# Attention, slot routing and a gated layer on one core: the first state link and its scaling are issued first in an iteration, the gate weights' scaled words right behind them on ScalarE

## The chip, the core and the metric

The kernel runs on one core of one Trainium2 chip. A core has five engines that run side by side, each through its own list in order: TensorE (PE, with its weight loads as PEld), VectorE (DVE), ScalarE (ACT), GpSimd (POOL) and SyncE (SP), which here issues nearly all loads. Engines wait for each other by semaphores. The metric is device microseconds of one execution; the time of before is the median of three runs.

## The reference, cut to what matters

```python
for t in range(S):                      # B=4, H=8, S=768, D=48
    state = alpha[:, :, t, :, None] * state + einsum('bhd,bhe->bhde', k[:, :, t], v[:, :, t])
    y[:, :, t] = einsum('bhd,bhde->bhe', q[:, :, t], state)
...
x = y laid out as (B * S, H * D)        # 3072 x 384
logits = x @ phi                        # 8 experts of 4 slots each: 32 columns
d = softmax of logits over tokens;  slot_input = d.T @ x
slot_out[e] = relu(slot_input[e] @ w1[e]) @ w2[e]
x = softmax of logits over slots @ slot_out
...
out = (silu(x @ w_gate) * (x @ w_val)) @ w_out      # float64 weights in memory
```

The weights of the last layer arrive as 64-bit floats, so the kernel has to make 32-bit floats of them from their words.

## The kernel before, in words

The work is in three stages. The first is a loop over `g` from 0 to 31 in the function `fast`: 16 pairs of heads (`n`), each in two halves (`h`) of three chunks of 128 tokens. The state of a pair is carried from chunk to chunk by a chain: TensorE adds the old state to a chunk's own product by a product with the identity (the **link**, L402 in `emit_st`), and ScalarE multiplies the sum by the chunk's decay and writes the new state to SBUF (the **scaling**, L404). The next link reads what the scaling wrote. An iteration holds two links that stand near its start (`emit_st(g, 1 - h)` and `emit_st(g, 2 - h)`); between them stand the score products of the next half (`emit_s`, L353, twelve passes). In odd iterations a third is issued later.

Around that chain an iteration does this. VectorE runs two decay scans for the half three further on (L306 to L314 in `scan_w` and `scan_p`) and masks the next half's scores (L360 in `emit_masks`). GpSimd scales keys and queries (L325) and masks the other head's scores (L363). ScalarE copies keys (L374), tokens (L466), scores (L362) and the output of the half (L434 in `emit_ip`). TensorE also adds the past's and the half's own part of the output (L420, L432) and forms logits (L453). The scores lie in two PSUM banks that are used again in each iteration, so the score products of an iteration need the masks and copies of the one before.

Into the same loop the conversion of the 24 gate-weight parts is woven, one part an iteration: `conv_y` (ScalarE, L249, the **scaled words**) writes a scratch of 128x384; VectorE makes the number of it in three steps, `conv(0)` (L253), `conv(1)` (L257, reads the scratch) and `conv(2)` (L261, reads it last). A part is loaded one or two iterations ahead (`pump_gv`, L244). Iterations 0, 1, 11, 12, 19, 20, 27 and 28 have none. A batch is four pairs of heads, so eight iterations; behind its end ScalarE also takes exponentials of the logits and copies them (L488, L490, L494 in `slot_steps`). They are issued at the end of iterations 8, 16 and 24, behind L434, and so stand ahead of the words and the first scaling of iterations 9, 17 and 25.

Everything is issued in the order in which the code is written; there is no scheduler. Each engine keeps that order. Loads go out on SyncE in the order of the calls, and a load into a region waits until its last reader is done. After the loop come the slot routing and experts (L853, L910), fed by weight loads (L236) into memory that the loop frees, and then the last layer (L1006 to L1045).

Of the kernel before, what the change touches and what calls it, by code (L numbers as in the profile page):

```python
# [34 lines left out]
GV0, RATE = 1, 840  # L35
# [57 lines left out]
def attention_slots_mlp(ctx: ExitStack, tc: tile.TileContext, kq, at, vt, phi, w1, w2, wgv, wo, cst, out):  # L93
# [47 lines left out]
    def program(general):  # L141
# [30 lines left out]
        def view(r, rows=128):  # L172
            o = r[0] % FAR
            return (near_t if r[0] < FAR else far_t)[0:rows, o:o + r[1]]

        def drop(r):
            ar.free(*r)
# [27 lines left out]
        def pump_units(limit=100):  # L205
            while uloads and limit:
                limit -= 1
                nm, i = uloads[0]
                z, n = {"a": (z_a, HW), "p": (z_p, HB), "v": (z_v, 288)}[nm]
                if not z:  # L210
                    return
                r = have[uloads.pop(0)] = (z.pop(0), n)
                if nm == "v" or i > 1:
                    load_unit(nm, i, r)

        def load_unit(nm, g, r):
            n, h = sgs[g]
            if nm == "a":
                nc.sync.dma_start(out=view(r), in_=at[units[n]][:, 387 * h:387 * h + HW])
            elif nm == "v":  # L220
                nc.sync.dma_start(out=view(r), in_=vt[units[n]][:, 288 * h:288 * h + 288])
            else:
                nc.sync.dma_start(out=view(r), in_=kq[units[n]][:, HB * h:HB * h + HB])
# [23 lines left out]
        def to_f32_y(raw, i=0):  # L247
            y = view(z_c[i])
            nc.scalar.activation(y, raw[:, 1::2], AF.Copy, scale=2.0 ** -112)  # L249
            return y  # L250
# [24 lines left out]
        def conv_y():  # L275
            i = gvd[0]
            if i < NG and ("wgv", divmod(i, 4)) in have:
                gvy[i] = to_f32_y(view(have["wgv", divmod(i, 4)]))
# [23 lines left out]
        def scan_w(g, between=lambda: None):  # L302
            n, h = sgs[g]
            wreg[g] = ((z_w.pop(0), HW), have.pop(("a", g)))
            w, a = (view(x, 112) for x in wreg[g])
            nc.vector.memset(rst[:, ::129], 1.0)  # L306
            nc.vector.tensor_tensor_scan(w[:, ::-1], a[:, ::-1], rst[:, ::-1], 0.0, ALU.mult, ALU.add)  # L307
            between()
            nc.vector.tensor_tensor(out=tots[:, n, 3 * h:3 * h + 3], in0=w[:, 1:387:129], in1=least, op=ALU.max)  # L309
            nc.vector.reciprocal(rst[:, 0:387:129], tots[:, n, 3 * h:3 * h + 3])  # L310
# [5 lines left out]
        def scale(g, which, eng):  # L316
            o = 2 - which
            if not which:
                pair[g] = have.pop(("p", g))
                kp[g], qp[g] = ((pair[g][0] + x, 384) for x in (0, 384))  # L320
            xv = view((kp, qp)[which][g], 112).rearrange("p (c t) -> p c t", t=CH)
            r = wreg[g][which]
            sv = view(r, 112)[:, o:o + 1]
            sv = bass.AP(sv.tensor, sv.offset, [list(sv.ap[0]), [129, 3], [1, CH]])
            eng.tensor_tensor(out=xv, in0=xv, in1=sv, op=ALU.mult)  # L325
            if g + (2, 4)[which] < NSG:
                (z_w, z_a)[which].append(r[0])
            else:
                drop(r)
# [6 lines left out]
        def nk(g):  # L336
            return 3 if sgs[g][1] == 0 else 2
# [39 lines left out]
        def new_g():  # L377
            ng[0] += 1
            return gsts[:, ng[0] % 7, :]
# [15 lines left out]
        def emit_st(g, c):  # L395
            if c >= nk(g):
                return
            n, h = sgs[g]
            cc = 3 * h + c + 1
            ps = dps[g][0:112, c * 48:c * 48 + 48]  # L400
            for p in (slice(0, 64), slice(64, 112)) if cc > 1 else ():
                nc.tensor.matmul(dps[g][p, c * 48:c * 48 + 48], lhsT=ident[p, p], rhs=gst[n, cc - 1][p, 0:48], start=False, stop=True, skip_group_check=True)  # L402
            gst[n, cc] = new_g()
            nc.scalar.mul(gst[n, cc][:, 0:48], ps, tots[:, n, cc:cc + 1])  # L404
            if c == nk(g) - 1:
                del dps[g]
# [164 lines left out]
        def keep_warm(n, p=None):  # L571
            if p is None:
                p = ps_y.tile([128, 512], F32, tag="y", name="warm")
            for _ in range(n):
                nc.tensor.matmul(p, lhsT=cold[0][:, 0:128], rhs=cold[0], start=True, stop=True)

        def fast():
            pump_units(4)

            def first_loads(h):  # L580
                for nm in "ap":
                    load_unit(nm, h, have[nm, h])

            first_loads(0)
            nc.scalar.dma_start(out=cs, in_=cst[:, 0:289])
            first_loads(1)
            nc.scalar.dma_start(out=phs, in_=phi)
            pump_units()
            calm, cold[0] = cold[0], view((z_g[0], 256)).bitcast(BF16)
            nc.gpsimd.memset(cold[0], 0.0)  # L590

            keep_warm(10)
            cold[0] = calm
            nc.vector.memset(rst, 0.0)
            nc.vector.memset(least, TINY)
            nc.gpsimd.memset(gsts, 0.0)
            scan_w(0)
            scale(0, 0, nc.gpsimd)
            scan_p(0)
            scale(0, 1, nc.vector)  # L600
            for c in range(3):
                emit_s(0, c)
            emit_kt(0)
            del kp[0]
            scan_w(1)
            scale(1, 0, nc.gpsimd)
            scan_p(1)
            keep_warm(4)
            scale(1, 1, nc.vector)
            emit_masks(0)  # L610
            emit_dh(0)
            emit_st(0, 0)
            pump_units()
            scan_w(2)
            scan_p(2)
            scale(2, 0, nc.gpsimd)
            scale(2, 1, nc.vector)
            pump_units()
            keep_warm(6)
            pend = []  # L620
            credit[0] = 0
            for g in range(NSG):
                n, h = sgs[g]
                nxt = g + 1 < NSG
                if g + 3 < NSG:
                    scan_w(g + 3, lambda: conv(0))
                    scan_p(g + 3)
                else:
                    conv(0)
                if g and g + 2 < NSG:  # L630
                    scale(g + 2, 0, nc.gpsimd)
                    scale(g + 2, 1, nc.gpsimd)
                conv(1)

                emit_st(g, 1 - h)
                if nxt:
                    for c in range(3):
                        emit_s(g + 1, c)
                emit_st(g, 2 - h)
                if nxt:  # L640
                    emit_kt(g + 1)
                if g:
                    emit_xt(g - 1)
                if nxt:
                    emit_masks(g + 1)
                    del kp[g + 1]
                    pump_units()
                late = False
                if g:
                    emit_l(g - 1)  # L650
                    release(xt.pop(g - 1), z_x, g + 1)
                    p = sgs[g - 1][0]
                    if sgs[g - 1][1] == 1 and units[p][1] == NU - 1:
                        pend += slot_steps(units[p][0])
                        late = True
                        pend.pop(0)()
                if pend and not late:
                    pend.pop(0)()
                emit_past(g)
                if nxt:  # L660
                    emit_dh(g + 1)
                    if h:
                        emit_st(g + 1, 0)
                conv(2)
                emit_ip(g)
                if late:
                    pend.pop(0)()
                    pend.pop(0)()
                if GV0 <= g and (g < 8 or g % 8 not in (2, 3)):
                    conv_y()  # L670
                if gvd[0] == NG and z_c:
                    done_c()

                pump_gv()
                credit[0] = min(credit[0] + RATE, 2 * BLK)
                reserve[0] = 6 - len(gvb)
                while credit[0] > 0:
                    c = credit[0]
                    pump(1)
                    if credit[0] == c:  # L680
                        break
                pump_units()
            for r in z_t:
                drop(r)
            assert few[1] is not None
            pump()
# [495 lines left out]
```

## Time and profile before

| | |
|---|---|
| median of 3 runs | 394.04 us (393.09 to 395.3) |
| the profiled execution | 395.87 us, its span 394.1 us |
| busy: TensorE, weight loads | 372.6 us (95%), 278.1 us (71%) |
| busy: VectorE, ScalarE, GpSimd | 291.0 us (74%), 201.5 us (51%), 103.9 us (26%) |
| mean granted clock of TensorE | 0.986 |

The profile is one execution. The span goes from the first to the last instruction; the time has 1.8 us more around it. Busy shares are means over the whole span, and the three stages differ, so a stage has to be cut out before a share says anything about it. The loop's 32 iterations take from some 13 to 158 us. In the rows, PEld is TensorE's weight load, which is where a wait of a product shows first; an arrow in brackets names the instruction that ended an engine's idle time.

### The profile page before, as it was taken

How to read it: one execution, taken by the hardware profiler on the slowest of the kernel's cores; microseconds unless marked ns; L12 is line 12 of the kernel's file. 1: busy time of each engine (PE TensorE's matmuls, PEld its weight loads, DVE VectorE, ACT ScalarE, POOL GpSimd, SP SyncE). 2: the span in 40 equal slices, each digit the busy share in tenths (PEclk: the TensorE clock that was granted, in tenths of full speed). 3: DMA queues.
4: the chain of work that ended last, by engine and by line, in shares of the span. 5: the costliest groups of instructions: out<-in, count | busy, mean ns of one | idle time of the engine just before them, and what ended most of it. 6: DMA issues, size and time to landing. Idle time of an engine off the chain costs nothing.

```text
span 394.1 us, 8610 instructions
## 1 busy us (share of the span) xinstructions
PE 372.6 (95%) x3309; PEld 278.1 (71%) x3309; DVE 291.0 (74%) x566; ACT 201.5 (51%) x468; POOL 103.9 (26%) x105
## 2 busy tenths in 40 slices
PE   6999999998998998999799999999999999999992
PEld 3677767776776776434358868888888888888781
DVE  6999997997999773214598995767767877877550
ACT  1456665656466455423267655446445445446431
POOL 3378675788588741020300000000000000000000
PEclk8999999999999999999899999999999999999997
DMA  8899997999799849799900004104114114112002
GB/s 277 316 320 360 351 360 276 312 346 321 258 362 351 289 157 350 288 335 407 400 33 0 1 2 150 39 34 150 35 37 151 37 35 148 39 35 81 2 1 89
DMA packets 28627, 74.25 MB, mean 188 GB/s; under 512 B 3216, under 2 KB 11648, under 8 KB 28576
## 3 DMA queue, kind: packets, MB, share of 16 engines
q1 hardware_dynamic: 28256, 73.27, 52.3%
q8 instruction: 28, 0.46, 0.5%
q10 hardware_dynamic: 272, 0.21, 0.2%
q14 instruction: 23, 0.19, 0.1%
q0 software_dynamic: 48, 0.13, 0.1%
HBM read 68.87 MB, written 4.72 MB: 187 GB/s over the span
## 4 chain that ended last, share of the span: by engine, by line
PE 55%; DVE 6%; DMA 3%; ACT 3%; issue 2%; SPq 0%; DVEq 0%; ACTq 0%
PE m L1045 21%; PE acc L1045 11%; PE s L1006 4%; PE s L1007 4%; DMA near<-w 3%; PE s L853 3%; PE y L432 2%; PE y L420 2%; DVE near L1012 1%; DVE rnd L1020 1%; ACT near L249 1%; PE sw L975 1%; PE l L453 1%; PE m L402 1%; PE m L390 1%
## 5 line engine op out<-in xcount | busy, mean ns | idle before, releaser
L1045 PE MATMUL m<-rnd 128*128 128x512 f32 x432 | 129.2, 389 | 0.0
L1045 PEld LDWEIGHTS m<-rnd 128*128 128x128 f32 x432 | 81.1, 188 | 16.8
L1009 ACT ACTIVATE near<-s 128x512 f32<-128x512 f32 x72 | 43.1, 599 | 79.0 <-PE s L1006 77.3
L1045 PE MATMUL acc<-rnd 128*128 128x512 f32 x216 | 81.1, 392 | 0.8 <-DVE rnd L901 0.8
L325 POOL TENSOR_TENSOR far<-far 112x384 f32<-112x384 f32 x61 | 78.5, 1306 | 6.5 <-DVE tots L309 3.6
L1012 DVE TENSOR_TENSOR near<-near,s 128x512 f32<-128x512 f32 x72 | 49.4, 686 | 36.1 <-ACT near L1009 35.9
L1020 DVE TENSOR_TENSOR rnd<-near,rnd 128x512 fp32r<-128x512 f32 x72 | 49.4, 686 | 3.2 <-ACT rnd L1018 3.1
L1045 PEld LDWEIGHTS acc<-rnd 128*128 128x128 f32 x216 | 40.5, 188 | 10.3 <-DVE rnd L901 1.6
L1018 ACT CAST rnd<-near 128x512 fp32r<-128x512 f32 x72 | 44.3, 615 | 0.2 <-DVE near L1012 0.2
L404 ACT ACTIVATE far<-m,tots 112x48 f32<-112x48 f32 x80 | 24.1, 301 | 29.1 <-PE m L402 17.3
L307 DVE TENSOR_TENSOR_SCAN far<-far,r 112x388 f32<-112x388 f32 x32 | 30.8, 962 | 5.2 <-DMA far<-at 2.5
L353 PE MATMUL s<-far 64*128 64x128 f32 x384 | 30.6, 292 | 2.5 <-DVE r L306 2.1
L1116 DVE TENSOR_REDUCE amm<-near 112x1 f32<-112x768 f32 x32 | 30.3, 947 | 2.5 <-DMA near<-at 2.5
L363 POOL TENSOR_SCALAR_AFFINE_SELECT far<-far 128x384 f32<-128x384 f32 x32 | 19.1, 596 | 48.8 <-ACT far L362 48.8
L314 DVE TENSOR_TENSOR_SCAN far<-far,r 112x387 f32<-112x387 f32 x32 | 30.7, 959 | 1.1
L257 DVE SCALAR_TENSOR_TENSOR near<-near 128x384 uint32<-128x384 uint32 x36 | 24.2, 672 | 7.9 <-ACT near L249 7.0
L434 ACT COPY far<-y 112x384 f32<-112x384 f32 x32 | 15.3, 480 | 28.1 <-PE y L432 28.1
L432 PE MATMUL y<-far 128*48 128x128 f32 (+1 forms) x384 | 28.6, 274 | 0.0
L1006 PE MATMUL s<-rnd 128*128 128x512 f32 x72 | 28.3, 393 | 0.0
L1007 PE MATMUL s<-rnd 128*128 128x512 f32 x72 | 28.1, 391 | 0.0
L353 PEld LDWEIGHTS s<-far 64*128 64x128 f32 x384 | 24.4, 189 | 4.7 <-POOL far L325 2.6
L402 PE MATMUL m<-far,cs 64*64 64x48 f32 (+1 forms) x256 | 19.9, 229 | 6.5 <-ACT far L404 3.8
(163 smaller groups left out, 495.0 us busy)
## 6 DMA issues: line engine op xcount, KB each, us to landing
near<-w SPq DMA_DIRECT2D x18, 768.0 KB, 6.8
far<-kq SPq DMA_DIRECT2D x32, 384.0 KB, 4.8
far<-w SPq DMA_DIRECT2D x14, 768.0 KB, 6.7
near<-wgv SPq DMA_DIRECT2D x24, 384.0 KB, 5.4
far<-at SPq DMA_DIRECT2D x32, 194.0 KB, 4.7
near<-at SPq DMA_DIRECT2D x16, 339.1 KB, 3.3
far<-vt SPq DMA_DIRECT2D x32, 144.0 KB, 4.0
near<-wo SPq DMA_DIRECT2D x12, 384.0 KB, 8.7
```

What stands on the lines that cost most here:

```text
L307: nc.vector.tensor_tensor_scan(w[:, ::-1], a[:, ::-1], rst[:, ::-1], 0.0, ALU.mult, ALU.add)
L314: nc.vector.tensor_tensor_scan(a, a, rst[:, 0:387], 0.0, ALU.mult, ALU.add)
L325: eng.tensor_tensor(out=xv, in0=xv, in1=sv, op=ALU.mult)
L353: nc.tensor.matmul(sps[g][s][:, o:o + CH], lhsT=k[64 * s:64 * s + 64, t0:t0 + CH], rhs=q[64 * s:64 * s + 64, t0:t0 + CH], start=True, stop ...
L432: nc.tensor.matmul(ps[p, o], lhsT=v[:, c, 48 * s:48 * s + p.stop - p.start], rhs=smk[g, s][:, c], start=False, stop=True, skip_group_check ...
L1006: nc.tensor.matmul(pg, lhsT=swk[n][:, 128 * o:128 * o + 128], rhs=ctT[t % 4], start=True, stop=True)
L1007: nc.tensor.matmul(pv, lhsT=swk[n][:, 256 + 128 * o:256 + 128 * o + 128], rhs=ctT[t % 4], start=True, stop=True)
L1009: nc.scalar.activation(sg, pg, AF.Silu)
L1012: nc.vector.tensor_tensor(out=h_, in0=sg, in1=pv, op=ALU.mult)
L1018: nc.scalar.copy(hi, h_)
L1020: nc.vector.tensor_tensor(out=lo, in0=h_, in1=hi, op=ALU.subtract)
L1045: nc.tensor.matmul(p, lhsT=passes[j][0][:, sl], rhs=passes[j][1], start=(f == 0 and j == 0), stop=(f == NF - 1 and j == 2))
```

## The change

In an iteration of the loop, `emit_st(g, 1 - h)` (the first link and its scaling) is called first, ahead of the scans, the scalings of keys and queries and the conversion steps, which are for other engines. `conv_y` is called right behind it instead of at the end of the iteration before; the conditions are shifted by one, so the same iterations have words as before.

```diff
             for g in range(NSG):
                 n, h = sgs[g]
                 nxt = g + 1 < NSG
+
+                emit_st(g, 1 - h)
+                if GV0 < g and (g <= 8 or g % 8 not in (3, 4)):
+                    conv_y()
                 if g + 3 < NSG:
                     scan_w(g + 3, lambda: conv(0))
                     scan_p(g + 3)
...
                     scale(g + 2, 0, nc.gpsimd)
                     scale(g + 2, 1, nc.gpsimd)
                 conv(1)
-
-                emit_st(g, 1 - h)
                 if nxt:
                     for c in range(3):
                         emit_s(g + 1, c)
...
                 if late:
                     pend.pop(0)()
                     pend.pop(0)()
-                if GV0 <= g and (g < 8 or g % 8 not in (2, 3)):
-                    conv_y()
                 if gvd[0] == NG and z_c:
                     done_c()
```

The order of TensorE, VectorE, GpSimd and SyncE is the same in both kernels. Only ScalarE's differs, at 24 places. The first piece is ScalarE's order at the start of an ordinary iteration, with the numbers of the buffers behind the names (L404 is the scaling, L249 the scaled words, L434 the output's copy, L374 and L466 the copies of keys and tokens):

```order
 L404 ACTIVATE far_94<-m_405,tots_74 112x48
 L434 COPY far_94<-y_398 112x384
-L249 ACTIVATE near_78<-near_78 128x384
-L404 ACTIVATE far_94<-m_405,tots_74 112x48 x2
+L404 ACTIVATE far_94<-m_405,tots_74 112x48
+L249 ACTIVATE near_78<-near_78 128x384
+L404 ACTIVATE far_94<-m_405,tots_74 112x48
 L374 COPY far_94<-m_450 128x224
 L466 COPY far_94<-m_454 128x288
```

The words stood ahead of both scalings of the iteration and now stand between them. The second piece is ScalarE's order behind the end of a batch, where the exponentials (L490 is the last of them) and the logits' copy (L494) come first:

```order
 L490 ACTIVATE nmx_76<-nmx_76 96x1
 L494 COPY lt_1282<-l_787 96x256
-L249 ACTIVATE near_78<-near_78 128x384
-L404 ACTIVATE far_94<-m_1266,tots_74 112x48 x2
+L404 ACTIVATE far_94<-m_1266,tots_74 112x48
+L249 ACTIVATE near_78<-near_78 128x384
+L404 ACTIVATE far_94<-m_1266,tots_74 112x48
 L374 COPY far_94<-m_1313 128x336
 L466 COPY far_94<-m_1318 128x288
```

The first scaling still stands behind the exponentials and the copy, but no longer behind the words. The third piece is ScalarE's order in the last iteration, where no score products and no copy of keys follow:

```order
 L434 COPY far_94<-y_2198 112x384
-L249 ACTIVATE near_78<-near_78 128x384
-L404 ACTIVATE far_94<-m_2203,tots_74 112x48 x2
+L404 ACTIVATE far_94<-m_2203,tots_74 112x48
+L249 ACTIVATE near_78<-near_78 128x384
+L404 ACTIVATE far_94<-m_2203,tots_74 112x48
 L466 COPY far_94<-m_2225 128x288
 L434 COPY far_94<-y_2233 112x384
```

The move is the same here.

## Rows read from the trace of the kernel before

**Rows 1.** The page, busy us, share of the span and instructions.

```profile
PE 372.6 (95%) x3309; PEld 278.1 (71%) x3309; DVE 291.0 (74%) x566; ACT 201.5 (51%) x468; POOL 103.9 (26%) x105
```

**Rows 2.** The loop's stretch: length, busy PE, PEld, DVE, ACT, POOL, clock, DMA share, GB/s.

```profile
13.00:158.00 145.00, 138.20 (x2068) 105.38 (x2065) 124.75 (x280) 84.00 (x243) 93.30 (x89) 1.00 0.89 313
```

**Rows 3.** Waits from 12 to 158: us in total, times, longest us.

```profile
PEld m L402 <- ACT far L404: 11.0, 24, 1.2
...
DVE pall L517 <- PE m L512: 2.8, 2, 1.4
```

**Rows 4.** TensorE's timeline, iterations with words: start, us, line, shape, passes.

```profile
34.10 0.94 PE L353 MATMUL s<-far 64*128 64x128 f32 x12
...
38.67 0.94 PE L353 MATMUL s<-far 64*128 64x128 f32 x12
39.74 0.31 PE L402 MATMUL m<-far,cs 64*64 64x48 f32 x4
...
42.81 0.38 PE L353 MATMUL s<-far 64*128 64x128 f32 x2
```

**Rows 5.** ScalarE's timeline in the iteration that starts at 38.67.

```profile
38.93 0.57 ACT L249 ACTIVATE near<-near 128x384 f32<-128x384 f32 x1
39.39 0.30 ACT L404 ACTIVATE far<-m,tots 112x48 f32<-112x48 f32 x1
40.11 0.30 ACT L404 ACTIVATE far<-m,tots 112x48 f32<-112x48 f32 x1 [0.42 <-PE m L402]
```

**Rows 6.** TensorE's timeline, the iteration without words at 67.24.

```profile
67.24 0.94 PE L353 MATMUL s<-far 64*128 64x128 f32 x12
68.11 0.31 PE L402 MATMUL m<-far,cs 64*64 64x48 f32 x4
...
71.18 0.48 PE L353 MATMUL s<-far 64*128 64x128 f32 x3
```

**Rows 7.** ScalarE's timeline, the same iteration's second scaling.

```profile
68.47 0.30 ACT L404 ACTIVATE far<-m,tots 112x48 f32<-112x48 f32 x1 [0.67 <-PE m L402]
```

**Rows 8.** TensorE's timeline, second link behind a batch and in the last iteration.

```profile
90.56 0.31 PE L402 MATMUL m<-far,cs 64*64 64x48 f32 x4 [1.01 <-ACT far L404]
...
155.46 0.31 PE L402 MATMUL m<-far,cs 64*64 64x48 f32 x4 [0.98 <-ACT far L404]
```

**Rows 9.** ScalarE's timeline, the words and first scaling behind a batch.

```profile
89.77 0.55 ACT L249 ACTIVATE near<-near 128x384 f32<-128x384 f32 x1
90.21 0.29 ACT L404 ACTIVATE far<-m,tots 112x48 f32<-112x48 f32 x1
```

**Rows 10.** VectorE's timeline over two iterations (L306 begins one).

```profile
32.88 0.06 DVE L306 MEMSET r<- 112x4 f32 x1
...
36.36 0.80 DVE L261 SCALAR_TENSOR_TENSOR near<-near 128x384 uint32<-128x384 uint32 x1
...
40.06 0.53 DVE L257 SCALAR_TENSOR_TENSOR near<-near 128x384 uint32<-128x384 uint32 x1
40.51 0.55 DVE L360 TENSOR_TENSOR far<-s,cs 128x384 f32<-128x384 f32 x1
...
41.53 0.06 DVE L306 MEMSET r<- 112x4 f32 x1
```

**Rows 11.** Three stretches, columns as in rows 2.

```profile
30.00:60.00 30.00, 28.39 (x421) 21.60 (x422) 28.52 (x61) 19.00 (x55) 21.70 (x20) 1.00 0.99 358
...
144.00:147.00 3.00, 2.87 (x48) 2.26 (x46) 1.17 (x4) 1.56 (x5) 2.45 (x3) 1.00 0.00 0
...
180.00:195.00 15.00, 12.52 (x124) 4.99 (x116) 9.23 (x17) 4.89 (x10) 3.53 (x3) 0.89 1.02 408
```

**Rows 12.** The chain that ended last, behind the loop: start, us, what.

```profile
179.49 12.28 DMA near<-w
```

**Rows 13.** SyncE's timeline, the load of one part of gate words.

```profile
31.22 0.59 SPq L244 DMA_DIRECT2D near<-wgv x1
```

**Rows 14.** All loads of gate words, from issue to landing.

```profile
DMA to landing us min/median/max: 3.1/5.4/7.0
```

## The prediction

> **What bounds the kernel now.** I first read the page's busy times: TensorE works 372.6 of 394.1 us, every other engine much less [rows 1]. That is an average over stages, so I cut out the stage that the change touches, the attention loop: from 13 to 158 us TensorE is busy 138.20 of 145.00 us at full clock, VectorE 124.75, ScalarE 84.00 and GpSimd 93.30, and the DMA engines have a share of 0.89 [rows 2]. TensorE sets the pace, with VectorE and the loads close behind.
>
> Next I asked what TensorE waits for in the loop. The largest entry is the second state link: the weight load of L402 waits 24 times for L404 on ScalarE, 11.0 us in all [rows 3]. The loop converts 24 parts of the gate weights, so it has 24 instructions of L249: the same number.
>
> The timelines say why. In the iteration that starts at 38.67 (I count an iteration from its first score product, L353) ScalarE runs L249 at 38.93, then the first scaling L404 at 39.39, the second at 40.11 [rows 5]. TensorE issues the second link at 39.74, 1.07 us after the iteration's start, and the next iteration starts at 42.81, after 4.14 us [rows 4]. The iteration at 67.24 has no words: its second link comes after 0.87 us, the next iteration after 3.94 us [rows 6]. Both are first halves of a pair of heads with the same TensorE work. So the trace of before holds the experiment already: 0.20 us at the link, 0.20 us in the iteration, nothing given back later.
>
> **The change, part by part.** No instruction is added or removed. VectorE, GpSimd, TensorE and SyncE keep their order, so no DMA issue moves, and nothing is moved past another on SyncE's or GpSimd's queue. On ScalarE each of the 24 L249 goes behind the first L404.
>
> *Ordinary iterations with words, 20 of them.* L404 starts 0.46 us earlier (39.39 back to 38.93 [rows 5]). TensorE cannot use all of it, because its twelve score passes come first; the floor is the 0.87 us of the iteration without words. Each saves 1.07 − 0.87 = 0.20 us: 4.0 us.
>
> *Three iterations behind a batch of heads.* There ScalarE has the exponentials and the copy of the logits ahead of L249. L404 starts at 90.21 and would start at 89.77 [rows 9], and TensorE's second link stands 1.01 us waiting for it [rows 8], more than the 0.44 us to be had. 3 × 0.44 = 1.3 us.
>
> *The last iteration* has no score products, so nothing covers ScalarE: its link waits 0.98 us [rows 8]. L249's 0.46 us is saved whole: 0.45 us.
>
> *What L249 costs in its new place.* It now stands before the second L404. Without words ScalarE idles 0.67 us there for TensorE's link [rows 7]. L249 holds the engine 0.46 us from its start to the next one's [rows 5], so it fits with about 0.2 us over, and the second L404, which TensorE's later products read, is not late. If L249 were itself held (by its load, or by the previous group's last VectorE step, which reads the same scratch), all of ScalarE's later work would wait behind it; that is a rival below.
>
> *Later words.* L249 ends about 0.2 us later in its iteration. VectorE reads them in L257. In the iteration at 38.67 L257 starts at 40.06 [rows 10]; L249 would end near 38.93 + 0.2 + 0.57 = 39.7. No wait there.
>
> *What is late next: VectorE.* Its iterations start at 32.88 and 41.53, two in 8.65 us, 4.33 each [rows 10]; TensorE's at 34.10 and 42.81, two in 8.71, 4.36 each [rows 4]. With 0.20 saved TensorE needs 4.16, so VectorE falls 0.17 us behind in each. What this reaches first is the mask L360, which must free the score bank for the next iteration: it ends at 40.51 + 0.55 = 41.06, and the bank is wanted at 42.81, 1.75 us later. The longest run of ordinary iterations is seven: 7 × 0.17 = 1.2 us, under 1.75. Behind each batch of heads VectorE stands waiting for TensorE (L517, twice, 2.8 us together [rows 3]) and is level again.
>
> The Trainium skill (SBUF — State Buffer, "Who interferes with whom") says that a VectorE instruction with two SBUF inputs and a GpSimd instruction that reads SBUF block each other for a whole instruction. The rows agree in kind: two instructions of one shape, L261 and L257, take 0.80 and 0.53 us [rows 10].
>
> *The loads.* In 30 to 60 us they run at a share of 0.99 and 358 GB/s [rows 11]. The same bytes in 4.16 instead of 4.36 us are 375 GB/s. In 180 to 195, with long rows, 408 GB/s flow [rows 11], so the bounds of what this mix can reach are 358 and 408. At 358 each iteration leaves the loads 0.2 us later. The tightest words that I found were issued at 31.22 [rows 13], are landed at 38.2 by the longest time seen, 7.0 us [rows 14], and are read at 38.93 [rows 5]: 0.7 us spare, plus the 0.2 that L249 moves back. That is the fifth group; four earlier savings of 0.2 use up nearly all of it. I therefore take 0.3 us off for stalls at the end of the run of seven, from VectorE or loads (nothing if neither bites, 7 × 0.2 = 1.4 if all of the run's saving goes).
>
> *After the loop* the chain runs through weight loads: 12.28 us of DMA from 179.49 [rows 12]. A faster loop helps only if those loads start earlier too. Their queue runs empty first: no bytes at all between 144 and 147 us [rows 11], since SyncE waits there for memory that the loop frees. So the whole end moves with the loop.
>
> **Sum:** 4.0 + 1.3 + 0.45 − 0.3 = 5.45 us. The profiled execution, 395.87 us around a span of 394.1, would be 390.4; it lies 1.8 us above the median of the runs, 394.04, which becomes 388.6.
>
> **The rivals.**
> - *VectorE or the loads take over.* If VectorE's 4.33 holds in all 20 iterations, they gain 20 × 0.03 = 0.6 us plus at best one 1.75 us of slack, not 4.0: total 4.1 at best, 2.4 at worst, 390 to 391.7. If loads at 358 GB/s pace the eleven ordinary iterations of the two fullest stretches, 2.2 us are lost: 390.8. For: both are within 5% of the pace now. Against: the slack above, and the periods in which either is idle. By the Trainium skill (DMA: Bandwidth & Descriptors, "Where 436 GB/s comes from") HBM binds loads near 358 GB/s per core, which is this rival; the trace has 408 [rows 11] and so does not agree that it is a ceiling.
> - *The gain is lost behind the loop.* If the queue, not the freeing of memory, sets when the last expert weights land, 394 stays. Against: the empty queue at 144 to 147.
> - *Slower: the words hold ScalarE.* L249, ahead of the second L404, waits for its load or its scratch, and holds L404, L374, L466 and L362, which all feed TensorE. The first 0.2 us of such a wait are free. To end 2 us above before it must also eat the 5.8: (5.8 + 2) / 24 + 0.2 = 0.5 us in every iteration with words. That needs loads 1.2 us or more later than now in all of them (0.7 spare), not just in the full stretches. The time would be about 396.
>
> **How the numbers follow.** Forecast, the cover holds: 0.70. VectorE or loads take part of it: 0.16. Lost behind the loop: 0.09. Words hold ScalarE: 0.05. For the forecast alone 387.3 (the lowest run of before, 393.09, less 5.8) to 389.8. The range for 8 in 10 adds the first rival's cases up to 391.7, and 0.3 below for the runs' own scatter: 387.0 to 391.7. A measurement of this kernel tells about 0.5%, 2 us, from no change: faster means under 392.1. That is the forecast and nearly all of the first rival less a little for the runs' scatter: 0.82; same 0.13; slower 0.05.
>
> **What would show it.** Right: the wait of L402 for L404 falls from 11.0 us to some 2 or 3, left in the three batch iterations and the last; iterations with words start every 3.94 and 4.37 us in turn; ScalarE's idle time before the second L404 shrinks to 0.2; the loop ends near 152.5 instead of 158; loads after it start that much earlier. Wrong: L353 waiting for L360, or L249 for a load or L261 (then VectorE or the loads took over); the loop shorter and the last expert load landing no earlier than 191.8; the second L404 starting only when L249 ends. The sum fails above all if VectorE falls behind by more than 0.17 us an iteration, since it can lose time to GpSimd at places that the shifted order decides.

## The result and the profile after

| | before | after |
|---|---|---|
| median | 394.67 us (392.99 to 401.89, 16 runs) | 390.19 us (387.83 to 392.9, 16 runs) |
| ratio to before, 95% interval | | 0.9869 [0.9841, 0.9897] |
| the profiled execution, its span | 395.87 us, 394.1 us | 390.72 us, 389.0 us |

The 16 runs of before include the three that the prediction goes by. Ratios leave disturbed executions out, so a highest time can lie further off than a ratio suggests. By the ratio the kernel became 1.3% faster; the medians lie 4.5 us apart, 1.1%. Forecast were 388.6 us, with a range of 387.0 to 391.7.

The page of after, busy us, and TensorE's granted clock in 40 slices:

```profile
PE 371.4 (95%) x3308; PEld 278.9 (72%) x3309; DVE 291.2 (75%) x566; ACT 201.2 (52%) x468; POOL 100.8 (26%) x105
...
PEclk9879999999999999999999999999999999999998
```

The work is that of [rows 1]. In the second and third slice the clock is below full; the last section comes back to that.

Waits of after from 24 to 155 us, in total, times, longest:

```profile
PEld m L402 <- ACT far L404: 2.8, 4, 0.8
...
DVE csm L529 <- PE m L525: 1.1, 1, 1.1
```

In [rows 3] L402 waited 24 times for 11.0 us. Four waits and 2.8 us are left. VectorE's 2.8 us at L517 [rows 3] are gone from the list; of its waiting for TensorE 1.1 us at L529 and 0.5 at L360 are left.

TensorE's timeline in two iterations with words (start, us):

```profile
36.55 0.94 PE L353 MATMUL s<-far 64*128 64x128 f32 x12
37.42 0.31 PE L402 MATMUL m<-far,cs 64*64 64x48 f32 x4
...
40.92 0.94 PE L353 MATMUL s<-far 64*128 64x128 f32 x12
41.79 0.31 PE L402 MATMUL m<-far,cs 64*64 64x48 f32 x4
...
44.86 0.83 PE L353 MATMUL s<-far 64*128 64x128 f32 x10
```

The second link comes 0.87 us behind the start, as in the iteration without words [rows 6]; in [rows 4] it was 1.07. The iterations take 4.37 and 3.94 us.

ScalarE in the second of them:

```profile
41.18 0.31 ACT L404 ACTIVATE far<-m,tots 112x48 f32<-112x48 f32 x1
41.38 0.56 ACT L249 ACTIVATE near<-near 128x384 f32<-128x384 f32 x1
42.16 0.30 ACT L404 ACTIVATE far<-m,tots 112x48 f32<-112x48 f32 x1 [0.22 <-PE m L402]
```

L249 stands in the gap in front of the second scaling, and ScalarE still waits 0.22 us there for TensorE. Without words the gap was 0.67 [rows 7].

Behind a batch, and in the last iteration (TensorE, then ScalarE's first scaling behind the same batch):

```profile
90.33 0.31 PE L402 MATMUL m<-far,cs 64*64 64x48 f32 x4 [0.58 <-ACT far L404]
...
152.78 0.31 PE L402 MATMUL m<-far,cs 64*64 64x48 f32 x4 [0.55 <-ACT far L404]
```

```profile
89.72 0.35 ACT L494 COPY lt<-l 96x256 f32<-96x256 f32 x1
89.97 0.30 ACT L404 ACTIVATE far<-m,tots 112x48 f32<-112x48 f32 x1
90.17 0.54 ACT L249 ACTIVATE near<-near 128x384 f32<-128x384 f32 x1
```

The waits of 1.01 and 0.98 us [rows 8] are 0.43 shorter; what is left stands behind the exponentials and L494, and in the last iteration behind L434, which the change did not move.

VectorE's mask L360 early and late in the run of seven, with the last step of the conversion behind the second:

```profile
25.80 0.55 DVE L360 TENSOR_TENSOR far<-s,cs 128x384 f32<-128x384 f32 x1
...
47.12 0.55 DVE L360 TENSOR_TENSOR far<-s,cs 128x384 f32<-128x384 f32 x1
47.59 1.27 DVE L261 SCALAR_TENSOR_TENSOR near<-near 128x384 uint32<-128x384 uint32 x1
...
51.87 0.55 DVE L360 TENSOR_TENSOR far<-s,cs 128x384 f32<-128x384 f32 x1
```

The score products in front of the first and the last end at 25.24 and 50.17 (starts 24.30 and 49.23, each 0.94 long). The mask is 0.56 us behind them at first, 1.32 five iterations later and 1.70 in the last: VectorE does fall behind, 0.19 us an iteration from end to end, but unevenly. TensorE never waits for the mask, not even in iterations 17 and 25, where it was 2.78 us behind.

The loads, stretches with the columns of [rows 2], and the chain that ended last:

```profile
40.00:50.00 10.00, 10.00 (x158) 7.93 (x153) 9.60 (x20) 6.50 (x19) 8.56 (x9) 1.00 1.03 374
...
110.00:120.00 10.00, 10.00 (x164) 7.81 (x160) 9.67 (x21) 6.25 (x19) 9.08 (x8) 1.00 1.02 378
```

```profile
176.68 11.37 DMA near<-w
188.10 0.85 PE so L910 x8
```

Both stretches lie in runs of ordinary iterations. They move 374 and 378 GB/s, where before moved 348 and 367 in the same stretches. From 30 to 60, a stretch that also holds longer iterations behind a batch, after moved 357 and before 358 [rows 11]. In after's list of waits from 24 to 155 none is for a load. The last expert load is issued at 176.68 instead of 179.49 [rows 12], and TensorE goes on at 188.10 instead of 191.8.

**Where the time came from, between the two profiles.** From the start of iteration 2 to the start of the loop's last output copy (L434) before took 21.24 to 158.21, 136.97 us; after takes 24.30 to 155.53, 131.23. That is 5.74 us. The spans differ by 5.1, since the profile of after lost 3.06 us ahead of iteration 2 (24.30 − 21.24). Behind the loop it gained 0.9 us on the last expert load (12.28 to 11.37), and about 1.5 us at the products behind that load, where the profile of before had a granted clock of 0.50. 5.74 − 3.06 + 0.9 + 1.5 = 5.1. The last of these three differences comes from the clock, not from the order of the work, and so does most of the first (see the last section).

### The profile page after: what moved, and what is told of

It is laid out like the page before. It is cut to its first block, busy times and chain, and to the rows that moved or that the text cites. A ratio compares the mean times of both kernels' runs of the same rounds, so it can differ in the third digit from the quotient of the medians.

```text
span 389.0 us, 8609 instructions
## 1 busy us (share of the span) xinstructions
PE 371.4 (95%) x3308; PEld 278.9 (72%) x3309; DVE 291.2 (75%) x566; ACT 201.2 (52%) x468; POOL 100.8 (26%) x105
## 3 DMA queue, kind: packets, MB, share of 16 engines
HBM read 68.87 MB, written 4.72 MB: 189 GB/s over the span
## 4 chain that ended last, share of the span: by engine, by line
PE 81%; DVE 6%; DMA 3%; ACT 2%; issue 2%; POOL 1%; SPq 0%; DVEq 0%; ACTq 0%; POOLq 0%
PE m L1045 22%; PE acc L1045 11%; PE s L353 6%; PE y L432 6%; PE y L420 6%; PE s L1006 4%; PE m L402 4%; PE s L1007 4%; PE m L390 3%; PE m L371 3%; PE l L453 3%; DMA near<-w 3%; PE s L853 3%; PE m L462 2%; DVE near L1012 1%
## 5 line engine op out<-in xcount | busy, mean ns | idle before, releaser
L325 POOL TENSOR_TENSOR far<-far 112x384 f32<-112x384 f32 x61 | 74.5, 1240 | 8.8 <-DVE far L307 4.7
L404 ACT ACTIVATE far<-m,tots 112x48 f32<-112x48 f32 x80 | 24.3, 304 | 26.7 <-PE m L402 14.6
L353 PE MATMUL s<-far 64*128 64x128 f32 x384 | 30.8, 293 | 3.5 <-POOL far L325 2.2
L363 POOL TENSOR_SCALAR_AFFINE_SELECT far<-far 128x384 f32<-128x384 f32 x32 | 20.2, 631 | 47.3 <-ACT far L362 47.3
L257 DVE SCALAR_TENSOR_TENSOR near<-near 128x384 uint32<-128x384 uint32 x36 | 21.6, 599 | 11.3 <-ACT near L249 10.3
L434 ACT COPY far<-y 112x384 f32<-112x384 f32 x32 | 15.3, 480 | 28.3 <-PE y L432 28.3
L353 PEld LDWEIGHTS s<-far 64*128 64x128 f32 x384 | 24.7, 191 | 6.1 <-POOL far L325 4.5
L420 PE MATMUL y<-far 48*48 48x128 f32 (+1 forms) x320 | 24.9, 283 | 0.0
```

What stands on the lines that cost most here:

```text
L353: nc.tensor.matmul(sps[g][s][:, o:o + CH], lhsT=k[64 * s:64 * s + 64, t0:t0 + CH], rhs=q[64 * s:64 * s + 64, t0:t0 + CH], start=True, stop ...
L420: nc.tensor.matmul(yps[g][p, o], lhsT=gst[n, cc][p, 0:p.stop - p.start], rhs=q[p, o], start=(cc == max(1, 3 * h)), stop=False, skip_group_ ...
```

## The experiments

My theory was the prediction's: the words' place on ScalarE ahead of the first scaling cost 0.20 us in an ordinary iteration and 0.44 behind a batch. The rivals were that the order in which the link is called made the difference, that ScalarE's whole order was sensitive, or that the cover at VectorE was nearly gone. Diffs are against the changed kernel.

**The link called first, the words left where they were.**

```diff
                 emit_st(g, 1 - h)
-                if GV0 < g and (g <= 8 or g % 8 not in (3, 4)):
-                    conv_y()
...
                     pend.pop(0)()
+                if GV0 <= g and (g < 8 or g % 8 not in (2, 3)):
+                    conv_y()
```

> Half of the change: the first link and its scaling are called first in an iteration, the words stay at the end of the iteration before, so every engine's order is that of the kernel before. Theory (ScalarE's order alone makes the gain): the time of before, ratio 1.000 within 0.004, the second link 1.07 us behind an iteration's start. Rival (the earlier call of the link itself helps, through fewer or weaker waits): a good part of the 1.3% is there already, ratio below 0.993.

394.78 us, ratio to before 0.9992 [0.9955, 1.0029]. In its trace L402 waits 24 times, 10.9 us, and the iterations start every 4.14 and 4.57 us. In the trace every engine's order is that of before. Calling the link first gives nothing that these runs show; the 24 exchanges on ScalarE are what the change gains by.

**The words behind both scalings.** The step that reads them, `conv(1)`, moves behind them in the code; VectorE's order stays.

```diff
                 emit_st(g, 1 - h)
-                if GV0 < g and (g <= 8 or g % 8 not in (3, 4)):
-                    conv_y()
+                words = GV0 < g and (g <= 8 or g % 8 not in (3, 4)) and gvd[0] < NG and ("wgv", divmod(gvd[0], 4)) in have
+                if words:
+                    gvy[gvd[0]] = view(z_c[0])
...
-                conv(1)
...
                 emit_st(g, 2 - h)
+                if words:
+                    conv_y()
+                conv(1)
```

> The words one place further: behind both scalings, ahead of the copy of the keys. Theory (they are free only in the gap of 0.67 us between the two scalings): the link keeps its 0.87 us, but the copies of keys, tokens and scores behind the words start about 0.28 us later, TensorE waits that much longer for the copy of the scores, and 23 iterations lose 0.1 to 0.28 us each against the changed kernel: 2 to 6 us above it, ratio to before 0.992 to 1.003. Rival (it matters only that the first scaling is not behind the words): the time of the changed kernel, ratio 0.987.

390.18 us, 0.9872 [0.9823, 0.992]: the same as the changed kernel. My expectation of a loss was wrong and the rival right. I had not looked at what the copies behind the words (L374, L466, L362) have to spare: TensorE's waits for them stay at 0.2 us each, and ordinary iterations still take 3.94 and 4.37. Only two iterations grew, 17 and 25, from 5.34 and 5.35 to 5.59 and 5.74: there the exponentials waited for VectorE, 0.15 and 0.31 us. That the later words had held VectorE up is not shown: in the profile with ten idle products (below), whose loop is the changed kernel's, iteration 25 took 5.69 us, and there too the exponentials waited for VectorE, 0.25 us. ScalarE in iteration 17:

```profile
86.33 0.47 ACT L488 ACTIVATE e<-l,nmx 96x256 f32<-96x256 f32 x1 [0.15 <-DVE nmx L481]
...
87.23 0.30 ACT L404 ACTIVATE far<-m,tots 112x48 f32<-112x48 f32 x1
87.95 0.30 ACT L404 ACTIVATE far<-m,tots 112x48 f32<-112x48 f32 x1 [0.42 <-PE m L402]
88.15 0.55 ACT L249 ACTIVATE near<-near 128x384 f32<-128x384 f32 x1
```

So the words need a place behind the first scaling; of the two tried there neither is better by more than these runs can tell.

**The exchange in ordinary iterations only**, and **in 9, 17, 25 and 31 only**: the first keeps the words ahead of both scalings in those four iterations, the second in all others.

```diff
+                words = GV0 < g and (g <= 8 or g % 8 not in (3, 4))
+                if words and g in (9, 17, 25, 31):
+                    conv_y()
                 emit_st(g, 1 - h)
-                if GV0 < g and (g <= 8 or g % 8 not in (3, 4)):
+                if words and not g in (9, 17, 25, 31):
                     conv_y()
```

> The change in the 20 ordinary iterations with words alone; in the three behind a batch and in the last one the words stay ahead of both scalings. Theory (the terms of the sum stand each by itself): 4.0 us less than before, less 0.3, ratio 0.990 to 0.991. Rival (VectorE or the loads eat the ordinary iterations' part and the batch iterations made the gain): ratio 0.995 or above.

> The complement: the change in the three iterations behind a batch and in the last one alone. Theory: 1.3 + 0.45 = 1.75 us less than before, ratio 0.9955. Rival (the ordinary iterations' part is eaten): the whole gain, ratio 0.988 or below.

391.01 us, 0.9899 [0.9864, 0.9934], and 393.12 us, 0.994 [0.9911, 0.9968]. Their waits of L402 for L404, one line from each (12 to 158 us):

```profile
PEld m L402 <- ACT far L404: 4.5, 4, 1.2
```

```profile
PEld m L402 <- ACT far L404: 9.2, 24, 0.8
```

The first has iterations of 3.94 and 4.37, and 5.58 to 5.78 behind a batch; the second 4.14 and 4.57, and 5.15 to 5.34. Each part gives its share in the trace, and both appear in the time: 1.0% (4.0 us of 395 expected) and 0.6% (1.75 of 395 is 0.44%). Together they are 1.6%, the whole change 1.3%; each interval is 0.3% wide to either side, so the times don't tell a sum from its parts more closely. The traces do: from the start of iteration 2 to the last L434 the two took 132.95 and 135.19 us, 4.02 and 1.78 less than before's 136.97. Together that is 5.80, and the changed kernel's loop gained 5.74.

**No words in the loop.** 23 of the loop's 24 L249 are left out, so that the weights lack their low bits.

```diff
-                gvy[i] = to_f32_y(view(have["wgv", divmod(i, 4)]))
+                gvy[i] = to_f32_y(view(have["wgv", divmod(i, 4)])) if general or i == 0 else view(z_c[0])
```

> The changed kernel with 23 of the loop's 24 instructions of scaled words left out (VectorE reads the scratch of the first, so the gate weights' low bits are wrong). Theory (behind the first scaling they cost TensorE nothing): the loop as in the changed kernel, iterations of 3.94 and 4.37 us, time within 0.4% of it; only the three batch iterations cannot gain, since the words are behind the first scaling there too. Rival (the words still cost, through ScalarE or through VectorE's wait): more than 1.5 us below the changed kernel, ratio to before below 0.983.

390.46 us, 0.9852 [0.9808, 0.9896]. The iterations take 3.94, 4.37, and 5.15 to 5.33 behind a batch, as in the changed kernel. In their new place the words cost TensorE nothing that these traces show.

**More work for VectorE**: a fill of 128x192 in each iteration.

```diff
                 conv(1)
+                nc.vector.memset(ct_all[:, 18:24, :], 0.0)
```

> The changed kernel with one more VectorE instruction in each iteration, a fill of 128x192 (about 0.2 us by the 0.38 us of the fill of 112x388 at the start). It asks how much of VectorE's cover the change has used. Theory (VectorE falls 0.17 us behind in an ordinary iteration and 1.75 are to be had): with 0.37 us a run of four fits (1.5), the run of seven does not (2.6): 0.8 us lost there, and up to 1 us more behind the batches, so 1 to 2 us above the changed kernel; score products wait for the mask at the end of the run of seven. Rival (VectorE has little room left at all): 20 x 0.2 = 4 us above it. Second rival (VectorE catches up by itself, since its time per iteration depends on where GpSimd's scalings fall): nothing.

392.37 us, 0.9894 [0.984, 0.9948]. TensorE at the end of the run of seven:

```profile
51.98 0.49 PE L353 MATMUL s<-far 64*128 64x128 f32 x2
52.80 0.93 PE L353 MATMUL s<-far 64*128 64x128 f32 x10 [0.34 <-DVE far L360]
54.18 0.31 PE L402 MATMUL m<-far,cs 64*64 64x48 f32 x4 [0.45 <-ACT far L404]
```

ScalarE ahead of that link's scaling:

```profile
53.11 0.47 ACT L488 ACTIVATE e<-l,nmx 96x256 f32<-96x256 f32 x1 [0.76 <-DVE nmx L479]
...
53.83 0.30 ACT L404 ACTIVATE far<-m,tots 112x48 f32<-112x48 f32 x1
```

Iterations 7, 9 and 11 took 4.46, 6.02 and 4.93 us instead of 4.37, 5.15 and 4.69, 1.2 in sum; the shorter runs lost nothing. The mask was then up to 3.3 us behind the score products, where the changed kernel has 1.70 at that place. This is the predicted rival in part: L353 waits 0.34 us for L360, at the end of the run of seven and nowhere else. But the wait that ended last in iteration 9 is the link's for its scaling: the exponentials had stood 0.76 us waiting for VectorE's L479, and the scaling stands behind them. In iteration 11 ScalarE's L531 waited 1.25 us for VectorE's L530 in the same way. So most of the loss reached TensorE through ScalarE, a way that the prediction did not have. The intervals of this kernel and the changed one overlap; the trace alone tells them apart.

**Four idle products ahead of each of the last four expert steps**, against the clock of 0.50 behind the wait for the last expert load in the profile of before.

```diff
         for i in range(16 - LAST, 16):
+            keep_warm(WARM, pss())
             fc2(i)
```

> The changed kernel with four products on nothing (128x512 bf16, as the kernel has them elsewhere) ahead of each of the last four expert steps, where TensorE waits for weight loads. In the profile of before the granted clock is 0.50 right behind that wait (192 to 195 us), in that of the changed kernel 1.00. Theory (whether the clock falls there differs from run to run and makes up part of the spread): the upper half of the runs comes down by about 1.5 us, the lower half stays; median 0.5 to 1 us below the changed kernel, clock 1.00 behind the wait. Rival (the spread comes from the start of the loop alone, where the changed kernel's profile has the clock at 0.50 from 17 to 23 us): no difference, or up to 0.5 us more for the added products.

390.78 us, 0.9881 [0.9836, 0.9926]. No gain. In its profile the clock stayed at full speed there, but so it did in that of the changed kernel.

**Also the exponentials behind the first scaling.** What is left of L402's wait stands behind L488, L490 and L494 in iterations 9, 17 and 25. Here they are called in the next iteration, behind the first link, and L494 behind the second scaling.

```diff
                 emit_st(g, 1 - h)
+                behind = late
+                if behind:
+                    pend.pop(0)()
                 if GV0 < g and (g <= 8 or g % 8 not in (3, 4)):
                     conv_y()
...
                 emit_st(g, 2 - h)
+                if behind:
+                    pend.pop(0)()
...
-                if late:
-                    pend.pop(0)()
-                    pend.pop(0)()
```

> The changed kernel, with one thing more in iterations 9, 17 and 25: the first state link and its scaling now also come ahead of the exponentials (L488, L490), and the copy of the scores (L494) stands behind the second scaling; the scaled words (L249) stay between. Theory (TensorE's serial link and scaling is still what ends these three iterations): the waits of 0.58, 0.78 and 0.78 us of L402 for L404 that are left in them shrink to at most 0.2, the iterations start 0.4 to 0.7 us apart less (5.15, 5.34 and 5.35 become about 4.7), the time falls by 1.5 to 1.8 us below that of the changed kernel, ratio to the kernel before about 0.983 where the changed kernel has 0.987. Rival (VectorE, 2.78 us behind in iterations 17 and 25, or the later copies L494 and L374, hold TensorE one step on): the wait comes back in the same or the next iteration as a wait for L374, for the exponentials or for VectorE's L501, and the time stays within 0.5 us of the changed kernel's.

389.27 us, 0.9872 [0.9822, 0.9921]. TensorE in iteration 17:

```profile
85.36 0.94 PE L353 MATMUL s<-far 64*128 64x128 f32 x12
86.23 0.31 PE L402 MATMUL m<-far,cs 64*64 64x48 f32 x4
...
87.51 0.42 PE L453 MATMUL l<-far,phs 112*32 112x128 f32 x6 [0.24 <-ACT lt L494]
```

The link comes after 0.87 us and its wait is gone, but L453 now waits for L494, which frees its bank. The three iterations took 4.81, 5.00 and 5.00 us: 1.03 us saved of the 1.5 to 1.8 that I expected. The time does not tell this kernel from the changed one.

**L494 ahead of the words again**: both `pend.pop(0)()` behind the first link.

> The changed kernel with the first link and its scaling ahead of the exponentials in iterations 9, 17 and 25, as in the run with L494 behind the second scaling, but with the copy of the scores (L494) directly behind the exponentials and so ahead of the scaled words (L249). In that run the wait of L402 was gone in these iterations (they took 4.81, 5.00 and 5.00 us in place of 5.15, 5.34 and 5.35), but TensorE's L453 waited 1.2 us in all for L494, which frees the bank that it writes. Theory (that was the whole of what came back): L494 starts 0.64 us earlier, L453 waits no more, the second scaling comes 0.25 us later and has cover until L420 reads it, and the three iterations take 4.6 to 4.75 us; 0.6 to 1.2 us less than that run, 1.6 to 2.2 less than the changed kernel. Rival (the second scaling or VectorE, behind by 2.8 us there, is the next limit): the three iterations stay at 4.8 to 5.0 us with a wait for L404 or for VectorE, and the time is that run's within 0.4 us.

389.76 us, 0.9857 [0.9816, 0.9898]. L453 no longer waits for L494 and the three iterations take 4.69, 4.69 and 4.72, as expected. But 19 and 27 grow from 4.69 to 4.97 and 5.20. ScalarE in iteration 19:

```profile
99.32 0.36 ACT L531 ACTIVATE ct<-ct 128x192 f32<-128x192 f32 x1 [1.29 <-DVE ct L530]
99.59 0.28 ACT L404 ACTIVATE far<-m,tots 112x48 f32<-112x48 f32 x1
```

It stands 1.29 us waiting for VectorE's L530, and the next scaling stands behind that. Against the changed kernel 0.46 + 0.65 + 0.63 us are won and 0.28 + 0.51 given back two iterations on. VectorE is the next limit there, one step later than both of my theories looked.

**Ten idle products instead of six ahead of the loop**, alone, and with each of the last two kernels.

```diff
-            keep_warm(6)
+            keep_warm(10)
```

> The changed kernel with ten idle products instead of six in the last group ahead of the loop (L575). In the changed kernel's profile TensorE came to iteration 0 at 11.38 us, had nothing to do from 14.76 to 16.98, where iteration 1's scores waited for GpSimd's scaled keys (L325), and its granted clock was 0.50 from 17 to 23 us; in the profile of before it came at 13.06, waited 0.35 us and kept 1.00. Theory (the idle stretch is what the fall of the clock follows, and it is what the upper of the two groups of times of either kernel shows): four more products of 0.245 us take 1.0 us of the idle stretch, the clock stays at 1.00 from 17 to 23, the times of this kernel lie in one group near 389 us, median 1 to 1.5 us below the changed kernel's. Rival (the two groups come from elsewhere, or 1.2 us of idle time is enough for the fall): the times stay in two groups and lie 0 to 0.7 us above the changed kernel's.

> Both edits of this call together on the changed kernel. Theory: they touch different stretches, so the gains add: about 2.5 to 3.3 us below the changed kernel, near 387 us, ratio to the kernel before 0.980. Rival: neither gives anything or the one eats the other's gain, and the time is that of the changed kernel within 0.7 us.

> The same with ten idle products instead of six ahead of the loop. In the two runs with ten, one profile had TensorE idle for 1.37 us ahead of iteration 1 with the granted clock at 0.50 behind it, and iteration 2 at 23.08 us (24.30 in the changed kernel's profile, with 2.23 us idle), the other had no such fall. Theory: ten products shorten the loss when it falls there, by about 1.2 us, and cost 0.2 us when it doesn't, so the median is 0 to 1 us below the run without them. Rival: they give nothing, and the median is 0 to 0.5 us above it.

Alone 389.72 us, 0.9861 [0.9813, 0.9909]; with the exponentials behind the link and L494 behind the second scaling 389.16 us, 0.9839 [0.9788, 0.9889]; with both behind the link 388.54 us, 0.983 [0.9802, 0.9858]. The last is the best version found, though its interval still overlaps that of the changed kernel. The theory of one group of times did not hold: the six times of the first spread from 387.48 to 390.89. The second's profile shows the loss still there, smaller: iteration 2 begins at 23.08, with 1.37 us idle ahead of iteration 1 and the clock at 0.50 from 19 to 21.

## Why the prediction held, point by point

**The bound.** What the words cost was TensorE's wait for the scaling. Two runs show it from both sides: with the link alone called first, waits and time stayed; without the words, no iteration from the second on was over 0.02 us shorter than with the words moved.

**The ordinary iterations** measured what the sum has: 4.14 and 4.57 became 3.94 and 4.37, and in iterations 10, 18 and 26 some 5.44 became 5.24: 20 × 0.20 = 4.0 us.

**Behind a batch** 0.44, 0.43 and 0.43 (5.59, 5.77 and 5.78 became 5.15, 5.34 and 5.35), against 3 × 0.44. **The last iteration** gave 0.43 against 0.45.

**The 0.3 us taken off** was the term that did not occur. The loop gained 5.74 us; the sum without this term is 5.75. VectorE fell behind as forecast (0.19 an iteration, 0.17 predicted), and this did not reach TensorE; the experiment with the fill shows that there was more than the 1.2 us of the run of seven to spare. Of the loads I had taken the lower bound, 358 GB/s, as a pace that each iteration would lose 0.2 us to. They moved 374 and 378 GB/s, and nothing in the loop waited for them. The Trainium skill (DMA: Bandwidth & Descriptors, "Where 436 GB/s comes from") puts the limit near 358 GB/s for a core; these rows do not agree that this stops loads here.

**L249 in its gap** left 0.22 us over, as predicted. What I did not see is that the place is not tight at all: 0.2 us over at the second scaling, and still more at the copies behind, as the run with the words behind both scalings showed.

**Behind the loop** the whole end moved, and the last load landed earlier, so the rival of a gain lost there fell. The loop did not end near 152.5 but near 155.5, because this profile lost 3.06 us ahead of iteration 2; 155.5 − 3.06 is 152.5. The medians are 4.5 us apart where the loop gained 5.74 and 5.45 were forecast; the time itself came out 1.6 us above the 388.6, inside the range. The profiled loop has the whole gain, and the rest goes with the granted clock. The six runs of after with a mean clock of 0.994 or more took 387.83 to 388.45 us, median 388.2; the ten others, at 0.991 or less, took 389.25 to 392.9. The 23 runs of before at 0.994 or more, of those taken along with the experiments, have a median of 394.2. At like clock the two kernels are thus 6.0 us apart. The prediction had no term for the clock, and why it falls in one run and not in the next stays open.

## What to carry to other kernels

Where a chain runs to and fro between two engines, put in-order filler on the second engine behind the chain's step, into the gap in which that engine waits for the first; a few of the kernel's own iterations without the filler already show what that is worth. Before counting a loss for what the filler pushes back, read what each pushed instruction has to spare at its reader. And when the chain gets faster, look for the engine that was level only because it waited: here VectorE had room for this change, and not for the next one.

## What the runs showed of the hardware that I had not expected

The granted clock fell to 0.50, the lower level of 1.2 GHz, ahead of 200 us in all profiles but one, but not at the same place, and this can move a time by more than most of the edits. After's first iterations (TensorE's timeline, then stretches with the columns of [rows 2]):

```profile
16.98 1.74 PE L353 MATMUL s<-far 64*128 64x128 f32 x12 [2.23 <-POOL far L325]
```

```profile
15.00:17.00 2.00, 0.01 (x1) 0.04 (x1) 1.84 (x6) 0.25 (x2) 1.44 (x2) 0.93 0.96 343
17.00:19.00 2.00, 2.00 (x16) 1.71 (x16) 1.85 (x4) 0.00 (x0) 0.43 (x1) 0.50 1.00 323
19.00:21.00 2.00, 2.00 (x16) 1.31 (x16) 1.90 (x5) 1.29 (x4) 0.00 (x0) 0.50 0.90 305
21.00:23.00 2.00, 2.00 (x25) 1.67 (x27) 1.44 (x4) 0.23 (x1) 1.70 (x3) 0.50 0.63 253
```

TensorE stands idle for 2.23 us, and then the twelve score products take 1.74 us instead of 0.94. In before's profile the clock was already down from 7.5 to 10.9 us, under the products ahead of the loop, idle ones among them: those took longer, TensorE reached iteration 0 at 13.06 instead of 11.38, and did not run out of work. Between these two profiles, then, the earlier full clock goes with the slower start, by 3.06 us. But the idle stretch does not always bring the fall. The kernel with the exchange in 9, 17, 25 and 31 only has the same stretch ahead of the same products, and its clock stayed at full:

```profile
17.36 1.03 PE L353 MATMUL s<-far 64*128 64x128 f32 x12 [2.23 <-POOL far L325]
```

```profile
17.00:19.00 2.00, 1.64 (x21) 1.50 (x22) 1.80 (x6) 0.30 (x1) 0.79 (x1) 1.00 0.96 332
19.00:21.00 2.00, 2.00 (x39) 1.49 (x39) 1.90 (x4) 1.12 (x3) 0.65 (x2) 1.00 0.90 300
```

Its iteration 2 began at 21.82 us, 0.58 behind before's; by this comparison some 2.5 of the 3.06 us are the clock's. In others (before, and the one with L494 ahead of the words, among them) a fall stands at 184 to 196 us, around the last expert steps, between waits for loads. The kernel with the exponentials behind the link shows no fall ahead of 382 us, and its profiled execution took 387.9 us; but its first twelve score products, from 6.96 us, took 1.65 us instead of 0.94, so its clock rows may not tell all. Which place it takes is not tied to this change: the profile with the link alone has it under the idle products as before has, and so has that with the exchange in ordinary iterations only. After's times follow the mean clock, as above; before's do less so, since four of its runs at 0.989 or 0.990 took only 392.84 to 393.42 us. That the scatter of the times comes from this alone is not shown.

L261 of one shape took 0.54 to 1.27 us. [rows 10] had shown one of 0.80. Each of the long ones in the loops of the two profiles, six of 0.80 before and seven of 0.80 to 1.27 after, began while an L325 was running on GpSimd. VectorE's cover has to be counted with the long ones.
